# Fourth to sixth weight block converted at the end of the attention, and the factor 1/6 moved to the output

## The chip, the cores and the metric

The kernel runs on one core of one Trainium2 chip. Its time is the device time of one execution in microseconds (us). The core has five engines with a queue each: TensorE (PE, with the loads of its weights shown apart as PEld), VectorE (DVE), ScalarE (ACT), GpSimd (POOL, hardly used here) and SyncE (SP, which issues the DMAs). Each queue runs strictly in the order of the program. An instruction can wait for counts (semaphores) that other engines raise when they finish something.

## The reference

The program is an attention with a soft cap, followed by two feed-forward layers. All numbers are float32.

```python
def _attn_ref(q, k, v, cap):                    # 2 x 12 heads, 448 rows, 64 columns
    scores = cap * np.tanh(scale * q @ k.T / cap)
    attn = np.exp(scores - scores.max()) ; attn /= attn.sum() + 1e-09
    return attn @ v
def _moe_ref(x, w_in, w_out, s, b):             # layer 0: 896 x 768 -> 2048 -> 768
    r = np.maximum(x @ w_in, 0.0)
    return (s * (r * r) + b) @ w_out
def _moe2_ref(x, w_in, w_out):                  # layer 1: same sizes
    h = x @ w_in
    g = h * np.clip(h + 3.0, 0.0, 6.0) / 6.0
    return (g @ w_out)
```

## The kernel before

**Attention.** Twelve pairs of heads are worked through in 42 units (`N = 42`). A loop over steps `n` issues, for every unit, the scores (L264, L268), a tanh and an exp on ACT (L272, L277), the products with v (L287, L290) and sums on DVE (L299, L302). A dictionary `plan` hangs further work on a step: the divisors (`total_pair`, whose reciprocal is L341 on DVE), the scaling of a pair's output (`scale_x`, L353, and the copy that rounds it to its high part, L354), and the low part (`rest_x`, L358). The two parts of x, high and low, are the operands of the first layer.

**Weights.** Each product of the feed-forward layers is done as three products of rounded high and low parts (`matmuls`, L231: three matmuls of 448 columns for each block of 128 rows). A weight block arrives by a DMA as pairs of 32-bit words, and is rebuilt by a conversion: a rescale on ACT (`rescale`, L212), a shift on DVE (`shift`, L220), and then either the low bits on ACT and one merge on DVE (`low_bits` L216, `merge` L226, used for w_in), or two merges on DVE (used for w_out). Then `parts` splits the block into a high part (ACT, L495) and a low part (DVE, L497). Raw words lie in three buffers of the name `raw`; a further load waits until one of them is free.

**Early work.** Blocks 0, 1 and 2 of layer 0's w_in are converted while the attention runs (dictionary `early`, by step). Blocks 3, 4 and 5 are loaded into the three raw buffers in that time, and block 3 is rescaled in step 38. The first products, of batch 0 with blocks 0 to 2, are spread over the attention's last steps (`first_pieces`).

**Feed-forward.** From there on the order is the result of a planner (`Plan.order`). It knows tasks with an engine, an estimated cost, the tasks that they follow and the buffers that they take; it gives every task a due time from the products that need it, and fills each engine's queue in a simulated run. So a change of one task's cost or place moves many others. The order of the products on PE is written by hand, and the planner may only pull a later one ahead. Blocks 0 to 5 are multiplied plainly, 7 banks of PSUM taking turns; the later ones by Strassen's scheme in pairs (`strassen`): product p1 goes to bank a; `cp`, a copy on ACT (L621), brings that partial sum to bank bb; p5 goes to bank c and is copied out (`c5`, L624); p2 is added in bank a, p6 in bank bb; `d1` on DVE (L630) adds bb and the copy of c; p7 and p4 follow in bank bb, p3 in bank c. p2 and p6 wait for `cp`, p7 and p3 for `d1`. The sums of x that Strassen needs (T1 to T4) are made on DVE by `minus` (L657) and split by `split` (L441 on ACT, L444 on DVE). After w_in comes w_out in halves; the products of the first out blocks fill the places between p6, p7, p3 and p4 of the last pair.

**Activations** (`activation`): a Relu on ACT from the bank (L579), in layer 0 a scaled square on DVE (L582) and the split with the bias (L590, L596); in layer 1 a minimum with 6 and the factor 1/6 (L584), then the product with h (L585), then the split (L592, L598). The finished outputs of layer 1 are copied from their bank by ACT (L728) and stored by a DMA each (L729).

Of the kernel before, what the change touches and what calls it, by code (L numbers as in the profile page):

```python
# [25 lines left out]
CI = KD * 128  # L26
# [26 lines left out]
class Plan:  # L53
# [8 lines left out]
    def add(self, engine, cost, run, after=(), use=(), soon=None):  # L62
        t = Task(engine, cost, run, after, list(use), len(self.tasks))
        for u in t.use:
            u.left += 1
        for a in t.after:
            a.then.append(t)
        t.soon = soon
        self.tasks.append(t)
        return t  # L70
# [102 lines left out]
def attention_moe_moe(ctx: ExitStack, tc: tile.TileContext, qk, v, cap, w1i, w1o, s, b, w2i, w2o, out):  # L173
# [232 lines left out]
    def feed_forward(sb):  # L406
# [59 lines left out]
        def convert(src, n, bits, before, blocks, raw=None, stage=0):  # L466

            r = raw or res("raw")

            def tile_of():  # L470
                if r.tile is None:
                    r.tile = raw_tile()
                return r.tile
            f = add("DMA", n * 0.0024, lambda: load_raw(tile_of(), src, n), (), [r]) if raw is None else None
            land = add("WAIT", 0, None, ()) if False else f
            a = add("ACT", acts(n, True), lambda: rescale(r.tile, n, bits), [land, *before], [r]) if stage < 1 else None
            sh = add("DVE", dve2(n), lambda: shift(bits), [a, *before])
            if n == CI and BYTES[0] or n == CO and BYTES[1]:
                l = add("ACT", 0.0022 * n, lambda: low_bits(r.tile, n), [a, land], [r])
                m = add("DVE", dve(n), lambda: merge(r.tile, n, bits), [sh, l], [r])  # L480
            else:
                l = add("DVE", dve(n), lambda: merge(r.tile, n, bits, 0x80000000), [sh], [r])
                m = add("DVE", dve(n), lambda: merge(r.tile, n, bits, low=True), [l], [r])
            for k in blocks:
                w_users[k] += [t for t in (a, sh, m) if t is not None]
            return m
# [18 lines left out]
        def plain_pair(layer, f):  # L505

            old = w_region(0, 4)
            w, g = [], None
            for i in range(2):
                cols = flat[:, i * CI:(i + 1) * CI]  # L510
                m = convert(w_src(layer, 0, f + i), CI, cols, old, (2 * i, 2 * i + 1), early_raw.pop(f + i, None))
                g, tasks = parts("gA", cols, CI, [m], (2 * i, 2 * i + 1), i * CI, g)
                w.append((g, i * CI, tasks))
            return w

# [54 lines left out]
        def activation(layer, f, bi, c_psum, made, c_slot=None):  # L570

            src_res = c_psum or c_slot
            src = (lambda: c_psum.tile[:, :S]) if c_psum else (lambda: c_slot.tile)
            t = c_slot if (c_slot and layer == 0) else res("slot")
            soon = 1.5 if c_psum else 3.0

            def relu():
                o = t.tile if t is c_slot else t_of(t, F32)
                nc.scalar.activation(o, src(), AF.Relu, **({"bias": three} if layer else {}))  # L579
            a = add("ACT", acts(S, layer), relu, made, [src_res, t] if t is not src_res else [t], soon)  # L580
            if layer == 0:
                q = add("DVE", dve(S, True), lambda: nc.vector.scalar_tensor_tensor(out=t.tile, in0=t.tile, scalar=st, in1=t.tile, op0=ALU.mult, op1=ALU.mult), [a], [t])  # L582
            else:
                q = add("DVE", dve2(S), lambda: nc.vector.tensor_scalar(t.tile, t.tile, 6.0, 1.0 / 6.0, op0=ALU.min, op1=ALU.mult), [a], [t], soon + 1)  # L584
                q = add("DVE", dve(S), lambda: nc.vector.tensor_mul(t.tile, src(), t.tile), [q], [t, src_res], soon + 2)  # L585
            hi, lo = res("slot"), res("slot")

            def upper():
                if layer == 0:
                    nc.scalar.activation(t_of(hi, F32R), t.tile, AF.Identity, bias=bt)  # L590
                else:
                    nc.scalar.copy(t_of(hi, F32R), t.tile)  # L592

            def lower():
                if layer == 0:
                    nc.vector.scalar_tensor_tensor(out=t_of(lo, F32R), in0=t.tile, scalar=bt, in1=hi.tile.bitcast(F32), op0=ALU.add, op1=ALU.subtract)  # L596
                else:
                    nc.vector.tensor_sub(t_of(lo, F32R), t.tile, hi.tile.bitcast(F32))  # L598
            h = add("ACT", acts(S, layer == 0), upper, [q], [t, hi])
            l = add("DVE", dve(S, layer == 0), lower, [h], [t, hi, lo])  # L600
            G[f, bi] = Value(hi, lo, [h, l])
# [55 lines left out]
            t = add("DVE", dve(S, ps), lambda: nc.vector.tensor_sub(t_of(r, F32), x_of(), y_of()), after, [r, *use])  # L657
            return r, t

        early_raw = {i: held("raw", r) for i, r in raws.items()}  # L660

        gs = [held("gA", first_groups[0]), held("gA", first_groups[1])]
        old = []
        m3 = convert(None, CI, early_region(3), [], (6, 7), early_raw.pop(3), stage=1)
        _, t3 = parts("gA", early_region(3), CI, [m3], (6, 7), CI, gs[1])
        first_w = [(gs[i // 2], i % 2 * CI, t3 if i == 3 else []) for i in range(4)]
        fb = [new_bank(ps) for ps in first_ps]
        for f in range(FIRST):
# [22 lines left out]
        for layer in range(2):  # L691
            partial = {}
            for half in range(2):
# [6 lines left out]
                for mt in OUT_ORDER:  # L700
# [24 lines left out]
                    elif layer == 1:  # L725
                        for bi in range(B):
                            y = res("slot")
                            t = add("ACT", acts(S), lambda y=y, q=bank[bi]: nc.scalar.copy(t_of(y, F32), q.tile[:, :S]), made[bi], [y, bank[bi]], 1.0)  # L728
                            add("DMA", 1.0, lambda y=y, mt=mt, bi=bi: nc.sync.dma_start(out[mt][:, bi * S:(bi + 1) * S], y.tile), [t], [y], 3.0)  # L729
                    else:  # L730
                        j, q = mt % HK, [lambda r=r: r.tile[:, :S] for r in bank]
# [42 lines left out]
    with tc.manual_schedule():  # L774
# [25 lines left out]
        for i in range(FIRST):  # L800
            jobs = ((lambda i=i: rescale(raws[i], CI, early_region(i), i == 0), lambda i=i: shift(early_region(i)),
                     lambda i=i: merge(raws[i], CI, early_region(i), 0x80000000), lambda i=i: early_merge(i),
                     lambda i=i: early_upper(i, i == 0), lambda i=i: early_lower(i)))
            for j, job in enumerate(jobs):
                early.setdefault(((6, 7, 8, 9, 10, 11), (12, 13, 14, 15, 20, 21), (20, 21, 22, 23, 28, 29))[i][j], []).append(job)
        early[38] = [lambda: rescale(raws[FIRST], CI, early_region(FIRST))]

        plan = {}
        at_step = lambda n, what, *args: plan.setdefault(n, []).append((what, args))
# [4 lines left out]
                at_step(U * d + 17 + o, finish_x, 2 * d + o)  # L814
        for p in range(P - 2):
            at_step(U * (p // 2) + 6 + 3 * (p % 2), take, p)
        at_step(N, total_pair, P - 2)
        at_step(N + 2, scale_x, P - 2, nc.scalar.copy)
        at_step(N + 2, total_pair, P - 1)
        at_step(N + 2, rest_x, P - 2)  # L820
        for o in (4, 3):
            at_step(N + 3, scale_x, P - o, nc.scalar.copy)
        at_step(N + 4, scale_x, P - 1, nc.scalar.copy)
        for o in (4, 3, 1):
            at_step(N + 4, rest_x, P - o)
# [78 lines left out]
```

## Time and profile before

| | |
|---|---|
| time, median of 3 runs | 552.57 us (549.31, 552.57, 553.83) |
| the profiled execution | 548.67 us, of which the span from first to last instruction is 546.9 us |
| PE busy | 537.1 us (98%), 2673 matmuls |
| DVE busy | 426.2 us (78%), 641 instructions |
| ACT busy | 371.6 us (68%), 503 instructions |
| mean granted TensorE clock | 0.997 of full speed |

Attention takes the first 100 us of the span, layer 0 the time to about 310 us, layer 1 the rest. The busy shares are means over stages. PE stands so near to all of its span that what matters is the short stretches in which it does nothing, and the instruction that ended each.

### The profile page before, as it was taken

The numbers are of one execution on the slowest core, as the hardware profiler recorded it, in microseconds if no ns is written. First come the engines' busy times: TensorE is split into PE (matmuls) and PEld (weight loads), VectorE is DVE, ScalarE is ACT, GpSimd is POOL, SyncE is SP. The second block draws the span as 40 slices with busy tenths as digits, with TensorE's granted clock in tenths as the row PEclk, the third lists the DMA queues.
The fourth block names the chain that finished last, engine by engine and source line by source line (L and its number), as shares of the span: only waits on it lengthen the run. The fifth ranks groups of instructions, "written<-read, shape, count | busy, mean of one in ns | idle before, by whom it ended". The sixth has DMA issues, their size and how long they took to land.

```text
span 546.9 us, 6996 instructions
## 1 busy us (share of the span) xinstructions
PE 537.1 (98%) x2673; PEld 438.0 (80%) x2673; DVE 426.2 (78%) x641; ACT 371.6 (68%) x503; POOL 0.4 (0%) x5
## 2 busy tenths in 40 slices
PE   8999999999899999999999999999999999999997
PEld 3222224789799999999999999998999999989996
DVE  2689987899998565889988999999866488997600
ACT  6999994299664576798657778974457579764401
POOL 0000000000000000000000000000000000000000
PEclk9999999999899999999999999999999999999999
DMA  8833411042224533222245332222463322225311
GB/s 316 340 113 104 157 42 53 1 155 77 79 78 155 211 116 115 97 77 82 84 169 186 115 117 96 78 77 79 154 212 115 116 96 78 77 78 185 110 50 52
DMA packets 16860, 64.13 MB, mean 117 GB/s; under 512 B 2214, under 2 KB 4154, under 8 KB 16698
## 3 DMA queue, kind: packets, MB, share of 16 engines
q1 hardware_dynamic: 16680, 63.52, 34.0%
q8 instruction: 21, 0.34, 0.3%
q10 hardware_dynamic: 146, 0.16, 0.1%
q14 instruction: 13, 0.11, 0.1%
HBM read 60.88 MB, written 2.79 MB: 116 GB/s over the span
## 4 chain that ended last, share of the span: by engine, by line
PE 77%; DVE 13%; ACT 7%; issue 3%; ACTq 0%; DVEq 0%
PE pf L231 31%; PE pav L231 25%; PE pz L231 7%; PE ps L264 5%; PE pav L290 4%; DVE w L226 2%; ACT t L272 2%; DVE sl L585 2%; DVE gAl L497 2%; ACT raw L216 1%; ACT w L212 1%; DVE gBl L497 1%; DVE sl L657 1%; PE pav L287 1%; DVE sl L584 1%
## 5 line engine op out<-in xcount | busy, mean ns | idle before, releaser
L226 DVE SCALAR_TENSOR_TENSOR w<-raw,w 128x512 uint32<-128x512 uint32 (+1 forms) x131 | 97.1, 760 | 16.6 <-ACT raw L216 15.1
L231 PE MATMUL pf<-sl,gBh 128*128 128x448 f32 x328 | 93.1, 365 | 0.0
L231 PE MATMUL pf<-sl,gAh 128*128 128x448 f32 x268 | 76.1, 365 | 0.0
L212 ACT ACTIVATE w<-raw 128x512 f32<-128x512 f32 (+1 forms) x79 | 57.8, 759 | 20.1 <-DMA raw<-in_w2o 7.3
L231 PE MATMUL pav<-sl,gAh 128*128 128x448 f32 x248 | 70.8, 367 | 0.0
L231 PEld LDWEIGHTS pf<-sl,gBh 128*128 128x128 f32 x328 | 61.6, 188 | 4.9
L231 PE MATMUL pav<-sl,gBh 128*128 128x448 f32 x216 | 61.3, 365 | 0.0
L231 PE MATMUL pf<-sl,gBl 128*128 128x448 f32 x164 | 60.0, 366 | 0.6 <-DVE pf L630 0.6
L216 ACT ACTIVATE raw<-raw 128x768 uint16<-128x768 uint16 x29 | 55.7, 1969 | 0.0
L231 PEld LDWEIGHTS pf<-sl,gAh 128*128 128x128 f32 x268 | 50.3, 188 | 4.0
L220 DVE TENSOR_SCALAR w<-w 128x512 uint32<-128x512 uint32 (+1 forms) x80 | 37.5, 476 | 16.9 <-ACT w L212 16.7
L495 ACT CAST gAh<-w 128x1536 fp32r<-128x1536 f32 (+2 forms) x27 | 33.5, 1239 | 24.7 <-DVE w L226 13.7
L231 PEld LDWEIGHTS pav<-sl,gAh 128*128 128x128 f32 x248 | 46.9, 189 | 3.8
L497 DVE TENSOR_TENSOR gAl<-w,gAh 128x1536 fp32r<-128x1536 f32 (+2 forms) x27 | 39.1, 1448 | 13.7 <-ACT gAh L495 13.7
L495 ACT CAST gBh<-w 128x1152 fp32r<-128x1152 f32 (+1 forms) x26 | 28.7, 1104 | 30.6 <-DVE w L226 23.9
L231 PE MATMUL pf<-sl,gAl 128*128 128x448 f32 x134 | 48.9, 365 | 0.0
L231 PE MATMUL pav<-sl,gAl 128*128 128x448 f32 x124 | 45.6, 368 | 0.0
L231 PEld LDWEIGHTS pav<-sl,gBh 128*128 128x128 f32 x216 | 40.6, 188 | 3.2
L272 ACT ACTIVATE t<-ps 128x896 f32<-128x896 f32 x42 | 37.9, 902 | 5.6 <-PE ps L264 5.6
L497 DVE TENSOR_TENSOR gBl<-w,gBh 128x1152 fp32r<-128x1152 f32 (+1 forms) x26 | 33.5, 1287 | 9.5 <-ACT gBh L495 9.5
L277 ACT ACTIVATE t<-t 128x896 f32<-128x896 f32 x42 | 39.9, 950 | 1.2
L231 PE MATMUL pav<-sl,gBl 128*128 128x448 f32 x108 | 39.6, 366 | 0.6 <-DVE pf L630 0.6
(161 smaller groups left out, 937.9 us busy)
## 6 DMA issues: line engine op xcount, KB each, us to landing
raw<-in_w1i SPq DMA_DIRECT2D x16, 768.0 KB, 4.3
raw<-in_w1o SPq DMA_DIRECT2D x24, 512.0 KB, 3.7
raw<-in_w2i SPq DMA_DIRECT2D x16, 768.0 KB, 5.6
raw<-in_w2o SPq DMA_DIRECT2D x24, 512.0 KB, 3.5
rqk<-in_qk SPq DMA_DIRECT2D x11, 448.0 KB, 5.5
out<-sl SPq DMA_DIRECT2D x12, 224.0 KB, 1.9
rb<-rows SPq DMA_DIRECT2D x10, 224.0 KB, 3.7
va<-in_v SPq DMA_DIRECT2D x1, 1344.0 KB
```

Of the source, the lines that this page charges most:

```text
L212: nc.scalar.activation(bits, up, AF.Copy, scale=2.0**-112)
L216: nc.scalar.activation(by[:, :, 2], by[:, :, 1], AF.Copy, scale=2.0**-13, bias=0.5**14 - 0.5)
L220: nc.vector.tensor_scalar(bits, bits, 3, None, op0=ALU.logical_shift_left)
L226: nc.vector.scalar_tensor_tensor(out=bits, in0=part, scalar=29 if low else mask, in1=bits, op0=ALU.logical_shift_right if low else ALU.bit ...
L231: nc.tensor.matmul(ps[:, :S], w[a], rhs[r], start=start and i == 0, stop=stop and i == 2, skip_group_check=True)
L264: nc.tensor.matmul(ps[:, j, :S], raw_qk[p][rows, 1, c * 128:(c + 1) * 128], raw_qk[p][rows, 0, :], start=True, stop=True)
L272: nc.scalar.activation(u_t[n], u_ps.pop(n)[:, :, :S], AF.Tanh, scale=icap_r)
L277: nc.scalar.activation(u_t[n], u_t[n], AF.Exp, scale=cap_r)
L290: nc.tensor.matmul(pav[p][(top, end)[j], :S], va[bi][:, d, (2 * (p % 2) + j) * NC + c, :], u_t[n][:, j, :], start=(p % 2 == 0 and c == 0), ...
L495: nc.scalar.copy(g.tile[0][:, at:at + n], cols)
L497: c = add("DVE", dve(n), lambda: nc.vector.tensor_sub(g.tile[1][:, at:at + n], cols, g.tile[0][:, at:at + n].bitcast(F32)), [a], [g])
L585: q = add("DVE", dve(S), lambda: nc.vector.tensor_mul(t.tile, src(), t.tile), [q], [t, src_res], soon + 2)
```

## The change

There are three edits, and what the planner makes of them.

First, the rescale of blocks 4 and 5 and the low bits of blocks 3, 4 and 5 (all on ACT) are issued in the attention's last step, `N - 1`; the shift and merge of blocks 3 and 4 (on DVE) in step `N`. Only the shift and merge of block 5, and the splits, are left to the planner, and two raw buffers are free for it from the start. Second, the scalings of pairs 8 and 9 (`P - 4`, `P - 3`) come in step `N + 2`, ahead of the second reciprocal, and the low part of pair 10 right behind them. Third, in layer 1 the minimum and the product with h are one instruction, without the factor 1/6, and that factor is applied by the copy of the output.

```diff
@@ convert()
-                l = add("ACT", 0.0022 * n, lambda: low_bits(r.tile, n), [a, land], [r])
+                l = add("ACT", 0.0022 * n, lambda: low_bits(r.tile, n), [a, land], [r]) if stage < 2 else None
@@ plain_pair()
-                m = convert(w_src(layer, 0, f + i), CI, cols, old, (2 * i, 2 * i + 1), early_raw.pop(f + i, None))
-                g, tasks = parts("gA", cols, CI, [m], (2 * i, 2 * i + 1), i * CI, g)
+                if layer == 0 and f + i == FIRST + 1:
+                    ms = []
+                else:
+                    early_one = early_raw.pop(f + i, None) if layer == 0 else None
+                    ms = [convert(w_src(layer, 0, f + i), CI, cols, old, (2 * i, 2 * i + 1), early_one, 2 if early_one else 0)]
+                g, tasks = parts("gA", cols, CI, ms, (2 * i, 2 * i + 1), i * CI, g)
@@ activation(), layer 1
-                q = add("DVE", dve2(S), lambda: nc.vector.tensor_scalar(t.tile, t.tile, 6.0, 1.0 / 6.0, op0=ALU.min, op1=ALU.mult), [a], [t], soon + 1)
-                q = add("DVE", dve(S), lambda: nc.vector.tensor_mul(t.tile, src(), t.tile), [q], [t, src_res], soon + 2)
+                q = add("DVE", dve(S), lambda: nc.vector.scalar_tensor_tensor(out=t.tile, in0=t.tile, scalar=6.0, in1=src(), op0=ALU.min, op1=ALU.mult), [a], [t, src_res], soon + 1)
@@ feed_forward()
-        early_raw = {i: held("raw", r) for i, r in raws.items()}
+        early_raw = {FIRST + 2: held("raw", raws[FIRST + 2])}
+        plan.sizes["raw"] = 2
-        m3 = convert(None, CI, early_region(3), [], (6, 7), early_raw.pop(3), stage=1)
-        _, t3 = parts("gA", early_region(3), CI, [m3], (6, 7), CI, gs[1])
+        _, t3 = parts("gA", early_region(3), CI, [], (6, 7), CI, gs[1])
@@ outputs of layer 1
-                            t = add("ACT", acts(S), lambda y=y, q=bank[bi]: nc.scalar.copy(t_of(y, F32), q.tile[:, :S]), made[bi], [y, bank[bi]], 1.0)
+                            t = add("ACT", acts(S, True), lambda y=y, q=bank[bi]: nc.scalar.activation(t_of(y, F32), q.tile[:, :S], AF.Copy, scale=1.0 / 6.0), made[bi], [y, bank[bi]], 1.0)
@@ the steps of the attention
+        home = {FIRST: FIRST, FIRST + 1: 0, FIRST + 2: 1}
+        def early_bits(i):
+            if i > FIRST:
+                rescale(raws[i], CI, early_region(home[i]))
+            low_bits(raws[i], CI)
+        def early_join(i):
+            shift(early_region(home[i]))
+            merge(raws[i], CI, early_region(home[i]))
+        early[N - 1] = [lambda i=i: early_bits(i) for i in home]
+        at_step(N, early_join, FIRST)
+        at_step(N, early_join, FIRST + 1)
         at_step(N, total_pair, P - 2)
-        at_step(N + 2, scale_x, P - 2, nc.scalar.copy)
+        for o in (2, 4, 3):
+            at_step(N + 2, scale_x, P - o, nc.scalar.copy)
+        at_step(N + 2, rest_x, P - 2)
         at_step(N + 2, total_pair, P - 1)
-        at_step(N + 2, rest_x, P - 2)
-        for o in (4, 3):
-            at_step(N + 3, scale_x, P - o, nc.scalar.copy)
```

The order of the matmuls on PE is the same as before from the first to the last, operand for operand; only buffers have other names. The order on DVE and ACT moves at many places. Three matter here. Lines of the changed kernel lie 3 or 4 further down than those of the kernel before.

The first place is the end of the attention on DVE, where `L302` is the last sum of the attention, `L341` the two reciprocals, `L353` and `L358` the scalings and low parts of x. A minus marks a row of before, a plus one of the change.

```order
 L302 TENSOR_TENSOR acc<-acc,t 128x896
+L220 TENSOR_SCALAR w<-w 128x768
+L226 SCALAR_TENSOR_TENSOR w<-raw,w 128x768
+L220 TENSOR_SCALAR w<-w 128x768
+L226 SCALAR_TENSOR_TENSOR w<-raw,w 128x768
 L341 RECIPROCAL rz<-pf 128x448
 L353 TENSOR_TENSOR xf<-pav,rz 128x448
+L353 TENSOR_TENSOR xf<-xf,rb 128x448 x2
+L358 TENSOR_TENSOR xl_93<-xf,xh_92 128x448
 L341 RECIPROCAL rz<-pz 128x448
-L358 TENSOR_TENSOR xl_93<-xf,xh_92 128x448
-L353 TENSOR_TENSOR xf<-xf,rb 128x448 x2
```

Two shifts and two merges now stand ahead of the first reciprocal, and two scalings and a low part ahead of the second instead of behind it. On ACT the three low bits and two rescales stand likewise between the last exp and the first `L354`.

The second place is ACT around the first Strassen pair (blocks 6 and 7 of layer 0), before its copy `cp`. Before:

```order
L441 CAST sl_1112<-sl_1018 128x448
L212 ACTIVATE w_70<-raw_949 128x512
L212 ACTIVATE w_70<-raw_1036 128x512
L441 CAST sl_1128<-sl_1025 128x448
L579 ACTIVATE sl_1131<-pf_790 128x448
L441 CAST sl_1137<-sl_1041 128x448
L495 CAST gBh_1157<-w_70 128x1024
L579 ACTIVATE sl_1171<-pf_826 128x448
L590 ACTIVATE sl_1173<-sl_1054,bt_67 128x448
L590 ACTIVATE sl_1179<-sl_1131,bt_67 128x448
L621 COPY pav_829<-pav_827 128x448
L212 ACTIVATE w_70<-raw_1060 128x512
```

And in the changed kernel, where `L624` is the copy `cp`:

```order
L495 CAST gBh_1111<-w_70 128x1024
L593 ACTIVATE sl_1125<-sl_1008,bt_67 128x448
L593 ACTIVATE sl_1131<-sl_1070,bt_67 128x448
L583 ACTIVATE sl_1136<-pf_803 128x448
L212 ACTIVATE w_70<-raw_1022 128x512
L212 ACTIVATE w_70<-raw_1105 128x512
L593 ACTIVATE sl_1154<-sl_1136,bt_67 128x448
L583 ACTIVATE sl_1171<-pf_835 128x448
L441 CAST sl_1178<-sl_1166 128x448
L441 CAST sl_1182<-sl_1173 128x448
L441 CAST sl_1188<-sl_1180 128x448
L624 COPY pav_838<-pav_836 128x448
```

The casts `L441` of the three T4 sums, which stood ahead of the high part `L495` of the first out block, now stand behind it and right ahead of the copy, and so do the two rescales `L212` of the second out block, which stood behind the copy. On DVE the three subtractions of T4 (`L660`, before `L657`) moved the same way: behind the low part `L497` of the first out block, one `L444`, one `L586` and three `L599`.

The third place is DVE in layer 1, ahead of the sum `d1` of the last Strassen pair of the first half (`L630` before, `L633` now). Before:

```order
L584 TENSOR_SCALAR sl_3084<-sl_3084 128x448
L585 TENSOR_TENSOR sl_3084<-sl_3073,sl_3084 128x448
L584 TENSOR_SCALAR sl_3098<-sl_3098 128x448
L585 TENSOR_TENSOR sl_3098<-pav_827,sl_3098 128x448
L497 TENSOR_TENSOR gAl_3093<-w_70,gAh_3092 128x1024
L584 TENSOR_SCALAR sl_3109<-sl_3109 128x448
L585 TENSOR_TENSOR sl_3109<-pf_726,sl_3109 128x448
L584 TENSOR_SCALAR sl_3126<-sl_3126 128x448
L585 TENSOR_TENSOR sl_3126<-pf_826,sl_3126 128x448
L220 TENSOR_SCALAR w_70<-w_70 128x512
L630 TENSOR_TENSOR pf_790<-pav_828,sl_3064 128x448
```

And now:

```order
L497 TENSOR_TENSOR gAl_3059<-w_70,gAh_3058 128x1024
L588 SCALAR_TENSOR_TENSOR sl_3080<-sl_3080,sl_3074 128x448
L588 SCALAR_TENSOR_TENSOR sl_3085<-sl_3085,pav_836 128x448
L601 TENSOR_TENSOR sl_3097<-sl_2961,sl_2994 128x448
L220 TENSOR_SCALAR w_70<-w_70 128x512 x2
L226 SCALAR_TENSOR_TENSOR w_70<-raw_2964,w_70 128x512
L588 SCALAR_TENSOR_TENSOR sl_3109<-sl_3109,pf_726 128x448
L226 SCALAR_TENSOR_TENSOR w_70<-raw_3050,w_70 128x512
L226 SCALAR_TENSOR_TENSOR w_70<-raw_2964,w_70 128x512
L588 SCALAR_TENSOR_TENSOR sl_3121<-sl_3121,pf_835 128x448
L633 TENSOR_TENSOR pf_803<-pav_837,sl_3052 128x448
```

Each pair `L584`, `L585` has become one `L588`, and three merges and one more shift of the second out block have come ahead of the sum. From the second w_in merge of the pair to the sum, eight activations lie in either kernel.

## Rows read from the trace of the kernel before

**Rows 1.** Timeline of PE, 104 to 117: start us, us, instruction, count, [idle <-releaser].

```profile
105.64 0.37 PE L231 MATMUL pf<-xh,gAl 128*128 128x448 f32 x1
106.33 0.47 PE L231 MATMUL pf<-xl,gAh 128*128 128x448 f32 x1 [0.32 <-DVE xl L358]
...
115.75 0.37 PE L231 MATMUL pav<-xh,gAh 128*128 128x448 f32 x1
116.19 0.47 PE L231 MATMUL pav<-xh,gAl 128*128 128x448 f32 x1
```

**Rows 2.** Timeline of PE at the first Strassen pair, 141 to 145.

```profile
141.43 0.56 PE L231 MATMUL pav<-sl,gAh 128*128 128x448 f32 x2
143.80 0.47 PE L231 MATMUL pav<-xh,gAl 128*128 128x448 f32 x1 [1.81 <-ACT pav L621]
144.11 0.36 PE L231 MATMUL pav<-xl,gAh 128*128 128x448 f32 x1
```

**Rows 3.** Windows behind that wait: stretch, busy us (count) by engine, PEclk, DMA, GB/s.

```profile
144.00:146.00 2.00, 2.00 (x8) 1.79 (x8) 2.00 (x5) 1.45 (x3) 0.00 (x0) 0.64 0.19 72
146.00:148.00 2.00, 2.00 (x7) 1.80 (x6) 2.00 (x4) 0.97 (x2) 0.00 (x0) 0.51 0.00 0
```

**Rows 4.** Timeline of PE in layer 1, last pair of either half.

```profile
369.41 0.57 PE L231 MATMUL pav<-sl,gAh 128*128 128x448 f32 x2
370.58 0.47 PE L231 MATMUL pav<-sl,gBl 128*128 128x448 f32 x1 [0.60 <-DVE pf L630]
...
480.90 0.47 PE L231 MATMUL pf<-sl,gBl 128*128 128x448 f32 x1 [0.61 <-DVE pf L630]
```

**Rows 5.** Timeline of ACT, 96 to 112 and 137 to 146.

```profile
98.65 0.57 ACT L354 CAST xh<-xf 128x448 fp32r<-128x448 f32 x1 [10.90 <-DVE xf L353]
...
108.88 1.97 ACT L216 ACTIVATE raw<-raw 128x768 uint16<-128x768 uint16 x1
...
140.71 1.05 ACT L495 CAST gBh<-w 128x1024 fp32r<-128x1024 f32 x1 [2.26 <-DVE w L226]
...
143.21 0.53 ACT L621 COPY pav<-pav 128x448 f32<-128x448 f32 x1
```

**Rows 6.** Timeline of DVE, 90 to 114 and 138 to 144.

```profile
91.58 1.09 DVE L302 TENSOR_TENSOR acc<-acc,t 128x896 f32<-128x896 f32 x1
95.00 2.96 DVE L341 RECIPROCAL rz<-pf 128x448 f32<-128x448 f32 x1 [2.33 <-PE pf L338]
...
100.70 2.96 DVE L341 RECIPROCAL rz<-pz 128x448 f32<-128x448 f32 x1 [2.09 <-PE pz L338]
...
107.26 0.55 DVE L220 TENSOR_SCALAR w<-w 128x768 uint32<-128x768 uint32 x1
...
109.57 1.70 DVE L657 TENSOR_TENSOR sl<-xf,sl 128x448 f32<-128x448 f32 x3
111.19 0.95 DVE L226 SCALAR_TENSOR_TENSOR w<-raw,w 128x768 uint32<-128x768 uint32 x1
...
112.53 1.87 DVE L582 SCALAR_TENSOR_TENSOR sl<-sl,st 128x448 f32<-128x448 f32 x3
...
142.32 1.22 DVE L497 TENSOR_TENSOR gBl<-w,gBh 128x1024 fp32r<-128x1024 f32 x1
```

**Rows 7.** Timeline of DVE in layer 1 ahead of the first of these two sums.

```profile
368.60 0.39 DVE L584 TENSOR_SCALAR sl<-sl 128x448 f32<-128x448 f32 x1
369.02 0.62 DVE L585 TENSOR_TENSOR sl<-pf,sl 128x448 f32<-128x448 f32 x1
...
369.89 0.63 DVE L630 TENSOR_TENSOR pf<-pav,sl 128x448 f32<-128x448 f32 x1
```

**Rows 8.** Groups by form, ACT and DVE: busy us, mean ns, idle before.

```profile
L212 ACT ACTIVATE w<-raw 128x512 f32<-128x512 f32 x48 | 30.6, 666 | 12.4 <-DMA raw<-in_w2o 7.3 <-DMA raw<-in_w1o 5.1
L226 DVE SCALAR_TENSOR_TENSOR w<-raw,w 128x512 uint32<-128x512 uint32 x96 | 63.7, 688 | 1.4
```

**Rows 9.** Waits of ACT: us in total, times, longest us.

```profile
ACT w L212 <- DMA raw<-in_w1o: 5.1, 3, 2.4
```

## The prediction

> **What bounds the kernel now.** The page comes first: PE is busy for 98% of the span, DVE and ACT for much less. Matmuls of the layers start 0.20 us apart (two take 0.56 us, of which one is 0.36 [rows 2]), so what can be won is only the time in which PE stands or runs slowly. I then asked for the waits of PE and looked at each in the timeline. In the layers there are five, and one stretch of low clock.
>
> Two are small. At 106.33 PE waits for a low part of x (L358) that comes late; the matmul should have started at 105.84, so 0.49 us are lost, and 0.10 more because the first matmul after a wait takes 0.31 us to the next instead of 0.20 [rows 1, 2]. At 116.19 it starts 0.24 late, plus 0.10 [rows 1]. Together 0.93 us.
>
> The large one is at the first Strassen pair. The second matmul of the row at 141.43 starts at 141.64, the next should follow at 141.84 and starts at 143.80, released by the copy `cp` on ACT: 1.96 + 0.10 us. The reader should see why the copy is late: ACT stood 2.26 us before the high part of the out block (L495), waiting for merges on DVE, with the copy queued behind [rows 5]. Behind the wait the granted clock is 0.64 in one 2 us window and 0.51 in the next, that is the lower level of 1.2 GHz for most of it; 0.36 x 2 + 0.49 x 2 = 1.7 us of work is lost [rows 3].
>
> Two are in layer 1: PE stands for 0.60 and 0.61 us before p7, released by `d1` on DVE [rows 4]. By the rows at 369.41 and 370.58 that is 0.76 + 0.10 us, so 0.87 each, 1.7 in all. DVE is simply late there: `d1` starts at 369.89 behind two activations and a shift [rows 7], although nine matmuls of an out block (9 x 0.20) have run since p6.
>
> In all 0.93 + 2.06 + 1.7 + 1.7 = 6.4 us. The order of PE doesn't change, so no more is to be had, and the question is which of these the new orders on DVE and ACT take away.
>
> **The work moved into the attention's end.** ACT gets three low bits of 1.97 [rows 5] and two rescales of 768 columns, which I price with 0.9, between the 0.67 of 512 columns [rows 8] and twice that: 7.7 us. It was idle for 10.9 us before 98.65 [rows 5], so this is covered with 3 us to spare. Without the cover the high parts of x would be late by as much. DVE gets two shifts of 0.55 and two merges of 0.95 [rows 6], 3.0 us, where it was idle for 2.33 before the first reciprocal; that starts at 91.58 + 1.09 + 3.0 = 95.7 instead of 95.00. Behind it come one scaling, and now two scalings and a low part more: instructions of this size start 0.54 apart in a run (three in 1.70, of which one is 0.62, an overlap of 0.08; [rows 6, 7]). So 95.7 + 2.9 + 4 x 0.54 = 100.8 against 100.70, where the second reciprocal waited for PE anyway. Cost: at most 0.1, and none on PE, which needs those parts only after 105.
>
> The three instructions taken from behind the second reciprocal bring everything after it forward by 1.6, less that 0.1: DVE reaches the shift of 107.26 at 105.8. The low part that PE waited for at 106.33 is then there at 104.8, and block 3, whose merge was at 111.19, needs none any more. Both small waits go: **0.93 us won**.
>
> **The copy cp in its new place.** Here the gain has to pass. I follow DVE from 105.8 to the copy by its order. In front of the low part L497 of the first out block (142.32 before, the next could start at 143.46) the queue has lost: the shifts and merges of blocks 3 and 4 (2 x (0.47 + 0.87) = 2.7, each less the overlap), the three subtractions of T4 (1.6), one L582 (0.60) and one L444 (0.54) [rows 6]. So DVE is through with it at 143.46 - 1.5 - 5.4 = 136.5. But now one L444, one L586 and three L599 (0.54 + 4 x 0.60 = 2.9) and only then the T4 subtractions follow: these start at 139.4 and the third ends at 141.2. The second and third cast on ACT wait for it by the counts in the program, and take 0.47 apiece, then the copy 0.53 [rows 5]: 142.8 to 142.9. PE, 0.93 earlier than before, wants it at 140.9. So the wait stays as long as it was, 2.0 us, with another cause: casts that nobody needs yet stand in front of the copy. PE goes on at 142.9 instead of 143.80: **0.9 us of gain is left**, with bounds 0 (the wait grows by what was won) and 3.0 (no wait).
>
> **The clock.** After a wait of the same length I expect the same fall and the same loss of 1.7; not counted as a gain. The Trainium skill (TensorE: Matmul & The Clock Gate, "What's actually happening") says that the gate's window runs free of the kernel, so that where a change falls varies from run to run. By that rule the same wait may pass without a fall, which would add the 1.7 us; no other wait of this trace shows it.
>
> **The fused activation in layer 1.** Before, an activation takes DVE from 368.60 to 369.56 (369.02 + 0.54): 0.96 us. The fused one has two tensor inputs; its nearest row is L582, 0.60 from start to start [rows 6], so 0.36 less, 11.5 us over 32 of them. DVE isn't the bound, so this counts at the two late sums alone. From the second w_in merge to the sum there are eight of them, 2.9 us less; but three merges (0.69 - 0.08 each, [rows 8]) and a shift of 512 columns (about 0.34) now stand ahead of the sum too, 2.2 more. Net 0.7 of the 0.87. If the fused form costs 0.54, like L585, the wait is gone; at 0.70 nothing is won. I take 0.8 each: **1.6 us**.
>
> **The factor at the output.** The last copy lies on the path behind the last matmul. As a scaled activation it costs between 0.53, the copy from PSUM [rows 5], and 0.67, a scaled activation of 512 columns [rows 8]: 0 to 0.14, I take 0.0, since both are one pass of ACT. The Trainium skill (ScalarE: Activation LUTs, "What ACT_TABLE_LOAD costs") gives 186 ns + 0.833 ns per column for immediate scale and bias, an estimate of 0.56 us here; by it the sum would be 0.03 smaller, and no row before shows that form from PSUM.
>
> **Sum.** 0.9 + 1.6 - 0.0 = 2.5 us. The profiled execution would go from 548.67 to 546.2. It lies 3.9 below the median of the runs shown, 552.57, for which I forecast **550.1**.
>
> **Rivals.** *The clock stays high* (0.20): as above but 1.7 better, 548.4. For it: the chance of where the wait falls; against it: the wait is no shorter than the one that was followed by a fall.
>
> *The whole 6.4 goes* (0.08): 546.2. DVE would have to reach T4 two microseconds earlier than I count. For it: ACT and DVE get 7.7 and 4.6 us of work out of the dense stretch; against it the order, with T4 and its casts ahead of the copy.
>
> *Layer 1 doesn't move* (0.14): the three merges ahead of the sum eat what the fusion saves; 0.9 remains, 551.7. For it: 0.7 against 0.87 is thin.
>
> *Slower: a DMA ahead of the copy* (0.08). The two rescales of the second out block, which stood behind `cp`, now stand ahead of it, and each waits for its words to land. The second one's buffer is freed only by a merge of the first out block near 133, four microseconds before ACT wants the words. Rescales have waited up to 2.4 us for such a landing [rows 9]. If it happens here, L593, L599, T4 and the copy shift by it: the wait grows from 2.0 to 4.4 and the low clock lasts twice as long, another 1.7. 2.5 - 2.4 - 1.7 gives 1.6 us slower, 554.2. It decides once the landing is over 2.5 late; less than that only eats the gain.
>
> The forecast keeps 0.50. All cases but the last lie between 546.2 and 551.7, and the three runs scatter by some 2 us around their median: the range is **546.0 to 553.0**. One per cent, 5.5 us, is about what a measurement of this kernel can tell. Faster by over 1% (below 547.0) needs the whole 6.4, or the high clock and a lucky scatter: 0.17. Slower by over 1% (above 558.1): 0.03. Within: 0.80.
>
> **What would show it.** The waits at 106 and 116 are gone and PE reaches the copy near 140.9: right or wrong for the moved work. A wait for L624 of about 2 us with three L441 straight ahead of it: right for the copy; under 1 us, or released by a landing, it is wrong. PEclk about 0.5 to 0.6 behind it. No wait for L633 in layer 1, and L588 at 0.62 to 0.68 us. If p7 still waits for L633, the term of 1.6 is wrong; if the whole span is shorter by over 4, the copy's term is.

## The result, and the profile after

The changed kernel takes 545.67 us (median of 12 runs, 544.61 to 553.43), the kernel before 552.31 (12 runs, 548.19 to 554.56); the ratio is 0.9907, 95% interval 0.9879 to 0.9934. (A ratio here is the comparison's own estimate with its interval, and not the quotient of the two medians, which is 0.988.) Timed once more beside the experiments it gave 546.27 against 549.75, ratio 0.995 (0.9918 to 0.9981). The forecast was 550.1, in a range of 546.0 to 553.0: the first median lies 0.3 us below that range, the second 0.3 inside it. The profiled executions differ by 3.5 us: 545.20 us with a span of 543.4, against 548.67 and 546.9. So three figures for one change, 6.6, 3.5 and 3.5; why the medians of the first comparison lie further apart than the traces is the second half of this story.

The waits of PE after (columns: who waits for whom, us in total, times, longest):

```profile
PE pz L795 <- DVE zeros L790: 1.4, 1, 1.4
PE pav L231 <- ACT pav L624: 1.1, 1, 1.1
PE ps L268 <- ACT t L272: 0.8, 1, 0.8
PE ps L264 <- ACT t L272: 0.5, 2, 0.3
```

Three of these lie in the attention and stood there before. Gone are the wait for the low part at 106 us and the late start at 116 [rows 1], and both waits of layer 1 [rows 4]. What is left is the copy `cp` (L624 now), 1.1 us where it was 1.8 [rows 2]. PE, ACT and DVE around it, from the timeline:

```profile
141.69 0.57 PE L231 MATMUL pav<-sl,gAh 128*128 128x448 f32 x2
143.34 0.47 PE L231 MATMUL pav<-xh,gAl 128*128 128x448 f32 x1 [1.07 <-ACT pav L624]
143.64 0.37 PE L231 MATMUL pav<-xl,gAh 128*128 128x448 f32 x1
...
138.98 0.55 ACT L583 ACTIVATE sl<-pf 128x448 f32<-128x448 f32 x1
140.62 0.57 ACT L441 CAST sl<-sl 128x448 fp32r<-128x448 f32 x1 [1.10 <-DVE sl L660]
141.82 1.03 ACT L441 CAST sl<-sl 128x448 fp32r<-128x448 f32 x2 [0.63 <-DVE sl L660]
142.76 0.52 ACT L624 COPY pav<-pav 128x448 f32<-128x448 f32 x1
...
139.97 1.82 DVE L660 TENSOR_TENSOR sl<-xf,sl 128x448 f32<-128x448 f32 x3
```

ACT waits twice for the T4 subtractions of DVE and does three casts ahead of the copy, as forecast. The copy ends at 142.76 + 0.52 = 143.28, where 142.8 to 142.9 was forecast. PE got there at 142.10, not 140.9, and so waited 1.24 + 0.10 us. Behind it the windows (busy us and counts of PE, PEld, DVE, ACT, POOL, then PEclk, DMA share, GB/s) show no low clock, where it was 0.64 and 0.51 before [rows 3]:

```profile
142.00:144.00 2.00, 0.93 (x5) 0.64 (x4) 1.90 (x4) 1.60 (x4) 0.00 (x0) 1.00 0.00 0
144.00:146.00 2.00, 2.00 (x12) 1.85 (x11) 2.00 (x6) 1.48 (x4) 0.00 (x0) 1.00 0.06 12
146.00:148.00 2.00, 2.00 (x12) 1.86 (x11) 2.00 (x5) 1.64 (x3) 0.00 (x0) 1.00 0.01 4
```

In layer 1, DVE and PE at the sum `d1` (L633) that was late at 370.58 [rows 4, 7]:

```profile
366.33 0.61 DVE L588 SCALAR_TENSOR_TENSOR sl<-sl,pf 128x448 f32<-128x448 f32 x1
366.86 0.62 DVE L633 TENSOR_TENSOR pf<-pav,sl 128x448 f32<-128x448 f32 x1
...
367.64 0.57 PE L231 MATMUL pav<-sl,gAh 128*128 128x448 f32 x2
368.05 0.36 PE L231 MATMUL pav<-sl,gBl 128*128 128x448 f32 x1
```

The fused activation takes 0.61 us and 0.53 from start to start; the sum ends at 367.48, 0.57 before p7 wants it.

Since PE's order is the same, each matmul of one trace can be set against the same matmul of the other. The change's lead over before grows or shrinks at these places only (us, + is later): start-up of the attention +0.51, the wait at 106 us -0.58, a slower row from there to 116 +0.17, the late start at 116 -0.33, a slower row from there to the copy +0.47, the copy -0.73, the clock behind it -1.56, 149 us +0.24, layer 1 -0.86 and -0.89. Together -3.5.

The start-up is not the work of the edits: it differs between two executions of one kernel. The same matmuls of the attention in the first and the second trace of the kernel before (the second is the first experiment below), and in the changed kernel:

```profile
6.91 1.02 PE L264 MATMUL ps<-rqk 64*128 64x448 f32 x4 [0.27 <-ACT t L272]
...
7.82 1.02 PE L264 MATMUL ps<-rqk 64*128 64x448 f32 x4 [0.27 <-ACT t L272]
...
7.42 1.02 PE L264 MATMUL ps<-rqk 64*128 64x448 f32 x4 [0.27 <-ACT t L272]
```

### The profile page after: what moved, and what is told of

Read it like the earlier page. It is cut to its first block, busy times and chain, and to the rows that moved or that the text cites. A ratio compares the mean times of both kernels' runs of the same rounds, so it can differ in the third digit from the quotient of the medians.

```text
span 543.4 us, 6960 instructions
## 1 busy us (share of the span) xinstructions
PE 535.9 (99%) x2673; PEld 437.6 (81%) x2673; DVE 414.7 (76%) x609; ACT 373.1 (69%) x503; POOL 0.4 (0%) x5
## 4 chain that ended last, share of the span: by engine, by line
PE 88%; DVE 7%; ACT 3%; issue 1%; DVEq 0%; ACTq 0%
PE pf L231 36%; PE pav L231 28%; PE pz L231 10%; PE ps L264 5%; PE pav L290 4%; ACT t L272 2%; DVE sl L660 1%; PE pav L287 1%; DVE w L226 1%; ACT t L277 1%; PE pz L309 1%; DVE sl L444 1%; PE pz L795 1%; PE ps L268 1%; DVE sl L586 1%
## 5 line engine op out<-in xcount | busy, mean ns | idle before, releaser
L231 PE MATMUL pf<-sl,gBh 128*128 128x448 f32 x312 | 88.6, 365 | 0.0
L231 PE MATMUL pf<-sl,gAh 128*128 128x448 f32 x284 | 80.7, 365 | 0.0
L231 PE MATMUL pav<-sl,gAh 128*128 128x448 f32 x280 | 79.6, 366 | 0.0
L212 ACT ACTIVATE w<-raw 128x512 f32<-128x512 f32 (+1 forms) x79 | 58.1, 760 | 21.5 <-DMA raw<-in_w2o 9.1
L231 PE MATMUL pf<-sl,gBl 128*128 128x448 f32 x156 | 57.0, 366 | 0.0
L231 PEld LDWEIGHTS pf<-sl,gAh 128*128 128x128 f32 x284 | 53.4, 188 | 4.1
L231 PEld LDWEIGHTS pav<-sl,gAh 128*128 128x128 f32 x280 | 52.6, 188 | 4.1
L495 ACT CAST gAh<-w 128x1536 fp32r<-128x1536 f32 (+2 forms) x28 | 34.4, 1228 | 29.2 <-DVE w L226 16.3
L231 PE MATMUL pav<-sl,gBh 128*128 128x448 f32 x184 | 52.3, 366 | 0.0
L497 DVE TENSOR_TENSOR gAl<-w,gAh 128x1536 fp32r<-128x1536 f32 (+2 forms) x28 | 40.2, 1440 | 15.4 <-ACT gAh L495 15.3
L231 PE MATMUL pav<-sl,gAl 128*128 128x448 f32 x140 | 51.2, 366 | 0.0
L495 ACT CAST gBh<-w 128x1152 fp32r<-128x1152 f32 (+1 forms) x25 | 27.7, 1107 | 24.6 <-DVE w L226 14.5
L497 DVE TENSOR_TENSOR gBl<-w,gBh 128x1152 fp32r<-128x1152 f32 (+1 forms) x25 | 32.2, 1289 | 15.1 <-ACT gBh L495 15.1
L231 PEld LDWEIGHTS pav<-sl,gBh 128*128 128x128 f32 x184 | 34.6, 188 | 2.7
L264 PE MATMUL ps<-rqk 64*128 64x448 f32 x144 | 34.3, 579 | 0.6 <-ACT t L272 0.5
```

What stands on the lines that cost most here:

```text
L212: nc.scalar.activation(bits, up, AF.Copy, scale=2.0**-112)
L231: nc.tensor.matmul(ps[:, :S], w[a], rhs[r], start=start and i == 0, stop=stop and i == 2, skip_group_check=True)
L264: nc.tensor.matmul(ps[:, j, :S], raw_qk[p][rows, 1, c * 128:(c + 1) * 128], raw_qk[p][rows, 0, :], start=True, stop=True)
L495: nc.scalar.copy(g.tile[0][:, at:at + n], cols)
L497: c = add("DVE", dve(n), lambda: nc.vector.tensor_sub(g.tile[1][:, at:at + n], cols, g.tile[0][:, at:at + n].bitcast(F32)), [a], [g])
```

## The experiments

The diffs here are shortened: operands and the planner's bookkeeping are partly left out.

**The kernel before, once more** (no edit).

> The kernel before, once more, unchanged. Its times in the first comparison lay in two groups, 548.2 to 550.0 and 552.2 to 554.6 us, and the profile that I read (548.67) is from the lower one; the change gains 3.5 us against that profile, but 6.6 between medians. Theory 1 (clock): the upper group is the same program with one or two more stretches of low clock behind its waits, 1.7 us each; a profile of the upper group then shows a granted clock below 1.00 behind a wait where the first trace had none (layer 1, or 106 us), and a mean clock of 0.993 or less. Theory 2 (something outside the waits, a start or a transfer): the mean clock is 0.997 again and the extra microseconds lie before 90 us or in one place that no edit touches. Ratio to itself 1.000 within 0.003.

551.6 us against 549.68, ratio 1.0014 (0.9986 to 1.0042). Its profile has a span of 551.5, 4.6 more than the first. The waits are the same but for a new late start at 150 us, which with the slow start behind it loses 0.38, and a shorter wait for the first d1 of layer 1 (0.26 lost, and not 0.86). The clock is 1.00 throughout: behind the copy's wait, as long as before, it did not fall, which gave back 1.56; the loss lies elsewhere. From start to start the matmuls take 202.7 ns on the mean in the first trace and 206.7 ns here, between the pauses at 150.5 and 374 and again behind 484 us. It shows as a count: the windows of PE (busy us and matmuls, PEclk, DMA share, GB/s), the kernel before first, then this run:

```profile
160.00:260.00 100.00, 100.00 (x496) 1.00 0.33 117
380.00:470.00 90.00, 90.00 (x446) 1.00 0.34 117
```

```profile
160.00:260.00 100.00, 100.00 (x486) 1.00 0.35 117
380.00:470.00 90.00, 90.00 (x446) 1.00 0.35 122
```

PE is 100% busy at full clock in all four rows, and does 2% less work in one. Neither theory had this. From here on, pace means this time from start to start.

**The fused activation alone**

```diff
-q = tensor_scalar(t, t, 6.0, 1.0 / 6.0, min, mult) ; q = tensor_mul(t, h, t)
+q = scalar_tensor_tensor(t, t, 6.0, h, min, mult)
-nc.scalar.copy(y, bank)
+nc.scalar.activation(y, bank, AF.Copy, scale=1.0 / 6.0)
```

> Only the activation of layer 1 in one instruction, and 1/6 in the output copy. My theory: the two waits for d1 in layer 1 go, 0.87 us each, everything before 300 us stays as before: 1.6 to 1.7 us faster than before (ratio 0.997), wait for the copy cp 2.0 and low clock behind it. Rival: all of the gain that the medians show beyond 3.5 us comes from these waits, since the clock falls behind them in most runs of before: then this edit alone gives 4 to 5 us (ratio 0.991 to 0.993).

Ratio 0.9995 (0.996 to 1.003), 546.76 to 554.75 us: the times alone show no gain. The trace gives what they hide: of PE's waits only those for d1 go, 0.86 and 0.88 us. So my theory holds in size there, and the rival of 4 to 5 us falls. One part of the theory missed: the copy's wait was as before, but the clock behind it stayed at 1.00.

**The moved work and the new order, without the fused activation** (the reverse of the diff above, on the changed kernel).

> The conversion of the three w_in blocks in the attention and the new order of the scalings, without the fused activation. My theory: no waits at 106 and 116 us (0.6 to 0.9), the wait for cp 1.1 to 2.0 us and no low clock behind it (1.7), both waits for d1 in layer 1 as before: 2.2 to 2.6 us faster than before in like runs. Rival: what the changed kernel won at cp it won by chance; then PEclk behind cp is 0.5 to 0.6 here and the gain is 0.9 to 1.2.

Ratio 0.9953 (0.9931 to 0.9976). The waits at 106 and 116 are gone, cp waits 1.2, and the clock behind it stays at 1.00, as my theory had it. Of the two waits for d1 only the second is back in full (0.6 us in the list of waits); the first, in a stretch at the slow pace, loses 0.28 us.

**The early conversion alone, and the order alone.** The second is this diff on the kernel before; the first is the rest of the moved work.

```diff
-at_step(N + 2, scale_x, P - 2) ; total_pair(P - 1) ; rest_x(P - 2)
-for o in (4, 3): at_step(N + 3, scale_x, P - o)
+for o in (2, 4, 3): at_step(N + 2, scale_x, P - o)
+at_step(N + 2, rest_x, P - 2) ; total_pair(P - 1)
```

> The kernel before, with the conversion of the three w_in blocks inside the attention, the old order of the scalings and the old activation. My prediction takes the wait at 106 us to come from the three instructions that stood ahead of the low part, which this kernel keeps, and the one at 116 from the merge of block 3, which it moves: the wait at 106 stays (0.5 us, the low part being no earlier), that at 116 goes, cp waits 1.1 to 2.2 us. Gain against before in like paces 0.2 to 0.9 us. Rival: the conversion is what carries the change; both waits go and cp waits 1.2 us as in the changed kernel.

> The kernel before, with the new order of the late scalings and nothing else. By the same reading the wait at 106 us goes here, since the low part comes ahead of the sums of x; the wait at 116 goes too if DVE is then early enough for the merge of block 3, which it still has to do. The wait for cp: 1.1 to 2.0 us. Gain 0.6 to 1.5 us in like paces, as much as both edits together. Rival: without the conversion in the attention the merges are late, the wait at 116 grows by as much as the one at 106 loses, and nothing is won.

Early conversion alone: ratio 1.0022 (0.9995 to 1.0049), so the 0.2 to 0.9 us that I expected did not come. Order alone: 0.9962 (0.9937 to 0.9987), more than I expected, 2.0 us between medians. Their waits, the conversion's first:

```profile
PE pav L231 <- ACT pav L625: 1.9, 1, 1.9
...
PE pf L231 <- DVE xl L358: 0.3, 1, 0.3
```

```profile
PE pav L231 <- ACT pav L621: 0.6, 1, 0.6
```

The order takes away both early waits by itself, and shortens the one at cp to 0.6 us, less than the 1.1 of the whole change. The conversion removes the late start at 116 and makes the copy later. So of the moved work the scaling order earns the gain; the DVE work that was put under the attention earns nothing that these runs can show. With it the planner places T4 and its casts straight ahead of cp; in the trace of the order alone two activations stand there instead.

**The order and the fused activation, without the conversion**

> The kernel before, with the new order of the scalings and the fused activation, but without the early conversion of the w_in blocks. Theory: the conversion inside the attention earns nothing, since with the order alone the waits at 106 and 116 us were gone and cp waited 0.76 us, against 1.2 to 1.4 in the changed kernel; so this one has no wait of d1 in layer 1, 0.7 to 0.8 us at cp, and 0.2 near 148, and in like paces it is 0.3 to 0.7 us faster than the change: lowest times about 544.1, median 544.5 to 546. Rival: the moved conversion frees 3 us of DVE that the layers need; then waits appear here that the changed kernel doesn't have, and the lowest times are 545.3 or more.

Median 546.58, lowest 544.27, against 546.27 and 545.03 for the change in the same comparison (below); ratios 0.9939 (0.9907 to 0.9971) and 0.995 (0.9918 to 0.9981). In the list cp waited 0.6 us, and its matmul started 0.78 late, as expected; no d1 was late. The rival falls, but the times, with four of twelve over 552, can't tell the two kernels apart.

**The copy ahead of the T4 casts** (on the changed kernel; the planner's list of what a task follows)

```diff
+if layer == 0 and f == PLAIN:
+    for v in ops["T4"]: v.tasks[0].after.append(cp)
```

> The changed kernel, with one more rule for the planner: the three casts of T4 come after the copy cp of the first Strassen pair. My prediction blamed these casts for the 1.4 us by which PE still waits at cp. If they are the cause, the wait goes and the kernel gains 1.0 to 1.4 us on the change (ratio to before lower by 0.002 to 0.0025). Rival: DVE as a whole is late here, busy without a gap from 129 to 146 us; then the copy comes in time, at 141.3 or earlier, but the next sum that PE needs, d1, is late by 1 to 2 us: the wait moves to about 148 us, the end stays within 0.4 us of the change.

Ratio 0.9932 (0.9909 to 0.9955), lowest 544.11. The copy is in time and the wait stands at d1:

```profile
PE pav L231 <- DVE pav L637: 0.9, 1, 0.9
```

Against the change, PE gained 1.33 us at cp and lost 0.94 at d1. The rival was right: the casts were only the nearest consumer of a DVE queue with hardly a gap (1.90 to 2.00 us busy in each 2 us of the windows above).

**No wait at all**

```diff
+for v in ops["T4"]: v.tasks[0].after[0].after.append(cp)   # the subtraction
+for t in uppers[-12:]: t.after.append(cp)                  # casts of activations
+t.after.append(first_d1[0])                # both merges, second out block
```

> The changed kernel with three more rules for the planner at the first Strassen pair: the T4 subtractions and the second casts of the last twelve plain activations come after the copy cp, and the merges of the second out block after the sum d1. With this order DVE and ACT should reach cp and d1 in time, so that PE has no wait at all between the attention and the end. Theory 1 (a wait costs its length): 1.2 to 1.6 us faster than the change, the times near 543.5 us. Theory 2 (the pace of the matmuls, 202.7 or 206.7 ns from start to start, is drawn anew at each pause of PE and kept until the next, and comes out of the attention at 206.7 in each of the traces so far, up to their next pause): with no pause the slow pace of 103 us stays to the end, 440 us x 2% = 8.5 us, less the 1.4 of the wait: the kernel is 6 to 7 us slower than the change, 551 to 553 us in most runs, with 206.7 ns throughout, although no engine waits for anything.

551.65 us (550.71 to 551.93): **slower than before**, ratio 1.0038 (1.0017 to 1.0059), and 5 to 6 us slower than the change in its two comparisons, with nothing waiting behind the attention. Theory 2 was right: the pace is 206.7 ns to the end. The same windows as above:

```profile
160.00:260.00 100.00, 100.00 (x485) 1.00 0.36 120
380.00:470.00 90.00, 90.00 (x438) 1.00 0.35 117
```

**One pause put back, at 147 us, or at 372 us.** On the kernel without a wait, `d1` of a single pair is computed three times over.

```diff
+for _ in range(3 if layer == 0 and f == PLAIN else 1):   # or: layer == 1 and f == HF - 2
     nc.vector.tensor_add(c, bb, s5)
```

> The kernel without a wait (the rules above), but the first Strassen pair's sum d1 is computed three times over, so that PE stands once for 0.3 to 1.3 us near 147 us and nowhere else. Theory 1 (a wait costs its length): 0.3 to 1.3 us slower than the same kernel without the pause. Theory 2 (a pause draws the pace anew): most runs come out of the pause at 202.7 ns; these are 6 to 8 us faster than the kernel without a pause, 543.5 to 545 us, and a few keep the slow pace, 551 to 553 us, with nothing between the two groups but scatter of 1 us.

> The kernel without a wait, with its sum d1 computed three times over in one pair only, the last pair of the first half of layer 1, so that PE stands for 0.2 to 0.9 us near 372 us. If a pause draws the pace anew and the pace before it is the slow one, the gain is in proportion to what is left behind the pause: 173 us x 2% = 3.4, less the pause: 548.3 to 549.2 us in most runs, 551.9 to 552.6 in the others; half of what the same pause gave at 147 us. Rival: what helped there was the relief of a queue near 147 us, and not the pause as such: then this kernel is 0.2 to 0.9 us slower than the one without a wait, 551.9 to 552.6 in all runs.

Adding idle time made the kernel faster: 546.31 us (544.38 to 548.58) with a pause of 0.4 us at 148.8. With 0.2 us at 371: 549.34, seven runs at 547.81 to 549.68 and five at 551.58 to 552.40. The early pause, then the late one:

```profile
160.00:260.00 100.00, 100.00 (x495) 1.00 0.37 122
380.00:470.00 90.00, 90.00 (x437) 1.00 0.33 113
```

```profile
160.00:260.00 100.00, 100.00 (x486) 1.00 0.37 122
380.00:470.00 90.00, 90.00 (x446) 1.00 0.35 117
```

The late pause wins about half of what the early one does, as its share of the remaining time says. The two clean groups that I expected of the early pause did not come: of its ten runs two lie in 543.5 to 545, eight from 545.46 to 548.58, and none at 551 or more. The trace, of the slowest of them, shows the fast pace end at 353 us, behind a single matmul that came 16 ns late, with no wait:

```profile
352.75 0.57 PE L231 MATMUL pf<-sl,gAh 128*128 128x448 f32 x2
353.16 0.38 PE L231 MATMUL pav<-sl,gAl 128*128 128x448 f32 x1
353.38 0.57 PE L231 MATMUL pav<-sl,gAh 128*128 128x448 f32 x2
```

Such a change without a wait puts runs between the two groups. But a start as late does not always do it: in four other traces at the fast pace six starts 10 to 20 ns late, two of them at this same matmul, changed nothing.

**The changed kernel once more**

> The changed kernel once more, beside the others. Lowest times 544.6, as in the first comparison. If the pace that is drawn at the last pause, near 149 us, decides, the times are in two groups: most at 544.6 to 546, a few at 552 to 553.5 (394 us x 2% = 7.8 more), none of them from a different wait; any trace shows 206.7 ns from 102 us to the wait for cp at 143. Rival: the pace changes with time on the chip and not at pauses; then a trace shows it change where PE doesn't stand, or the times fill the space between the groups.

545.03 to 553.70 us: six runs up to 545.76, four from 546.77 to 549.35, two over 552. The trace has 206.7 ns from 102 to 143 us, and no other wait than the first. The two groups are there, but the times also fill some of the space between them, as the rival says: the four would fit a change without a wait like the one above, but no trace shows one in this kernel, so this stays open.

**The row broken without a wait** (on the kernel without a wait, at 17 places from 168 us on)

```diff
-nc.tensor.matmul(ps[:, :S], w[a], rhs[r], ...)
+for lo, hi in ((0, cut), (cut, S)):
+    nc.tensor.matmul(ps[:, lo:hi], w[a], rhs[r][:, lo:hi], ...)
```

> The kernel without a wait again, but from about 168 us on, every 22 us one matmul of 448 columns is done as two (224 and 224, 320 and 128, 384 and 64 and so on, most of them twice, 17 places), so that the even row of starts is broken without any wait for another engine. Theory A (the pace belongs to PE alone, to how starts and weight loads fall against each other, and any break of the row may change it): the trace shows the pace go from 206.7 to 202.7 ns, or back, at some of the 17 places and nowhere else, and the times lie 1 to 6 us below the 551.7 of the kernel without a wait. Theory B (it takes a wait for another engine, the engine standing): 206.7 ns from end to end, and the 17 additional matmuls cost 0.05 to 0.2 us each: 552.5 to 555 us.

546.09 us (545.10 to 547.41), ratio 0.9927 (0.99 to 0.9953), where the same order without cuts had 1.0038. The first cut, in the timeline, has the 0.21 us steps ahead of it and 0.20 behind; then the windows:

```profile
168.06 0.37 PE L237 MATMUL pf<-sl,gBl 128*128 128x448 f32 x1
168.26 0.58 PE L237 MATMUL pf<-sl,gBh 128*128 128x224 f32 x3
168.69 0.36 PE L237 MATMUL pf<-sl,gBl 128*128 128x448 f32 x1
168.88 0.57 PE L237 MATMUL pf<-sl,gBh 128*128 128x448 f32 x2
```

```profile
160.00:260.00 100.00, 100.00 (x498) 1.00 0.38 123
380.00:470.00 90.00, 90.00 (x446) 1.00 0.36 118
```

(These windows hold 5 and 4 of the split matmuls, each counted twice.) No engine has to wait for another for the pace to change, as theory A has it; what in PE sets the pace no run shows. Of the 17 stretches behind a cut 16 ran at 202.7 ns; one (388 to 410, behind 352 and 96 columns) at 206.7, and the next cut ended it.

## Why the prediction was right, and where it wasn't

**Early waits** (0.93 forecast): right that both go, and right in size, 0.58 + 0.33 = 0.91 in the traces. The credit was put on the order for 106, and that is shown; for 116 I named the moved merge, and either edit alone removes it. What the forecast lacked is that behind the wait at 106 us PE ran on the faster row, in the trace that I read: without it the row stays slow up to the copy, which takes 0.64 back.

**The copy** (0.9 us ahead behind it, the early waits included): the place, the queue and the time were right. In the trace PE goes on at 143.34 and not 142.9, 0.46 ahead, since this execution started up 0.51 later. Less its start-up, PE goes on at 142.8 in both traces of the change and at 143.74 to 143.80 in three with the old orders (the kernel before twice, the fused activation alone): 0.98 ahead of the trace that I read. But "casts that nobody needs yet" was only the nearest cause: without them d1 is late instead.

**The clock** (loss of 1.7 stays): this step failed. I expected the same fall after a wait of the same length, 2.0 us; the wait was 1.34, since the slow row brought PE to it later, and the clock did not fall, worth 1.56. The runs show how fickle the old loss was. Counting those with a mean clock of 0.997 or less: 57 of 124 runs of the kernel before, in whose traces PE's starts lie 2.15 and 2.17 us apart at cp; 6 of 12 with the fused activation alone (2.15 us); 11 of 12 with the conversion alone (2.28 us); none of 118 runs of the nine kernels in which that distance was 1.60 or less. So in these counts the loss goes with the length of the wait, and at the old length it is a matter of the execution; why it falls in one and not in the next no run shows. The Trainium skill (TensorE: Matmul & The Clock Gate, "What's actually happening") says the gate's window runs free, so that a change may fall differently from run to run. 57 of 124 for one program agrees. My rival that the clock stays high was the case that came, and by a shorter wait, not by the chance that I gave for it.

**Layer 1** (1.6): 0.86 + 0.89 = 1.75, and 1.74 in the experiment with that edit alone. The fused form costs 0.53 from start to start, like the cheaper of my two bounds, so the rival of the three merges had no room. At the slow pace the first of the two waits is worth less: 0.26 us were lost at it in the second trace of the kernel before.

**The output** (0.0): the scaled copy takes 0.54 us, the plain one 0.53. Right. The prediction says that no row before shows this form from PSUM; the Relu of layer 0 (L579) does, with 0.54 us.

So 0.9 + 0 + 1.6 = 2.5 became 0.98 + 1.56 - 0.24 + 1.75 = 4.05, of which the later start-up took 0.51: the 3.5 between the traces. Against an execution of before whose clock holds, and which then loses 0.38 at 150 us, it is 0.98 + 0.14 + 1.75 = 2.9, near the forecast. With the fall in 57 of 124 the mean is some 3.4, an estimate from these traces for like pace and start-up.

**What no step had** is the pace, 202.7 or 206.7 ns, worth 2% of a stretch. In the traces it stays as it is until the row of matmuls breaks, by a pause, a cut or once a start 16 ns late, and a break may change it. All traces leave the attention at 206.7; behind 24 of the 34 pauses of over 0.1 us in them the pace was 202.7 (the pause with the low clock behind it is not counted). The kernel before has its last breaks at 150, 370 and 480 us, so its runs scatter over 548 to 555; the change has its last one at 149, and keeps what it gets there for 394 us, 7.8 us apart: 544.6 to 545.9, or 553.4, in the first comparison. There ten of its twelve runs came out fast, and eight of twelve of before were above 552: so of the 6.6 us between medians some 3 are the draw of the pace, by the estimate above. The second comparison's 3.5 is another draw. That the first median came out 4.4 under the forecast is so for the most part luck: of the pace, which the sum did not have, and of the clock, which it put at nothing.

## What to carry to other kernels

Before trusting a per cent between medians, count the matmuls in equal windows of the two traces: at the same clock and 100% busy a row may still run at two paces. Taking away the last small wait lost more here than the wait was worth, and splitting a matmul now and then was a cheap remedy; cuts nearer to the attention's end, on the version without the early conversion, were not run. And when a wait goes, look at which queue was full: here the wait only moved from one consumer of DVE to the next.

## What the runs showed of the hardware

- Matmuls of 448 columns in float32, each with its own weights, follow each other every 206.7 ns (steps of 206 and 207) or in a repeating row of 207, 202, 203, 202 and 199 ns, 202.7 on the mean, at a granted clock of 1.00. Once the second went over to the first behind a start 16 ns late; six starts as late, within 6 ns, changed nothing.
- Two matmuls of 224 columns in place of one of 448 cost 0.02 us here (0.10 + 0.11, and 0.21 to the next start, against 0.405 for two at the fast pace); 320 and 128 cost 0.05.
